# Products issued ahead of a run-time switch, scatters without order, and half of the last result sent before its last product

## The chip, the cores and the metric

The kernel runs on one core of a Trainium2 chip. The metric is the device time of one execution in microseconds; the median of several runs counts. The profile is of one execution.

## What is computed

Two blocks follow each other. The first is chunked attention over 4 batches, 8 heads and 768 positions with a head size of 64; its output, seen as 3072 tokens of 512 numbers, is the input `x` of the second. The second is a mixture of 8 experts in which each token goes to the one expert with its highest logit, and no token is dropped:

```python
expert_idx = np.argmax(x @ w_gate, axis=1)
for e in range(E):
    h = np.maximum(x_sorted[lo:hi] @ w1[e], 0.0)
    y_sorted[lo:hi] = h @ w2[e]
y = y_sorted[inv_perm]
return (gate_w[:, None] * y).astype(np.float32)
```

`w1` of an expert is 512x1024, `w2` is 1024x512, everything is float32. How many tokens an expert gets is known only when the kernel runs.

## The kernel before

**Attention and routing** fill the first 160 us or so. Each block's rows of `x` are scattered to a table in device memory, `x_dram`, with 1024 places for every expert. Counts per expert are turned into `cases`: the number of tokens in steps of 32.

**The experts** are a loop over `e`. For each, `tc.Switch(index[e], CASES)` chooses at run time one of 33 bodies, written out for 0, 32, 64 ... 1024 tokens. Every engine has its own copy of the code and makes the jump for itself, from registers that `loads` filled (line 1211). The code that follows the switch is common again: `result`, then the next switch. So at each boundary an engine jumps twice: from the end of the old body to the common code, and from there into the next body.

**A body** (`expert`) takes one part of tokens, or two equal ones if there are over 512. A part of `w` tokens is split into two halves of `hf = w // 2` columns, and each layer is a product of 2x2 blocks by Strassen's scheme in Winograd's form: seven products in place of eight, on blocks and sums of blocks. Products 1 and 2 (`product(1, ...)`, `product(2, ...)`) use the blocks as they are; products 3 and 5 to 7 need sums of `x` blocks (`xS`) or sums of weight blocks (`wT`), product 4 a sum of weights. `product` runs on TensorE (line 1081) into one of six accumulator banks of 2x256 columns. Each matmul of these float32 operands gives two records in the trace, so that one product of the first layer for one half of its outputs (`p`) is 8 records.

In `first_layer` the products come in the order 1, 2 (for both `p`), 6, 7, 5, 4, 3; the bank of each is the next of six in turn. ScalarE copies product 1 (line 1107), VectorE adds product 2 to it (line 1108), ScalarE applies the ReLU (line 1100). Between them stand `backs`: the four `put_back` of the expert before. `put_back` turns 128 tokens of the result back on TensorE (`turn_y`, line 1012), scales them with the gate on ScalarE (`gated`, line 1017, four buffers `y`), and scatters their rows to the output from GpSimd (`store`, line 1021). `turns` are the transposes of the next expert's `x` (`turn_x`, lines 1006 and 1007). `second_layer` runs products 1, 4, 5, 6, 7, 2, 3; the sums for the next expert are made in `between`. Product 3 is the last, in bank 5; VectorE adds it in `result` (line 1164), after the switch. This completes the first half of the token columns of `yT`; the other half is complete two additions earlier (lines 1156 and 1158), and `put_back` with `g` of 2 and 3 reads that half.

**Order.** The whole part is written under `manual_schedule`: each engine runs its instructions as the code issues them. Waits are put in by the recording layer from what each instruction reads and writes. It sees every `store` as a write to the whole of `out`, so each scatter waits for the one before to land. The last expert's result is put back after the loop, four `put_back` one after the other (lines 1251 and 1252). Then `good`, one number that says whether the fast path was admissible, is loaded into a register on each engine (line 1261), and a branch skips the fallback `general`.

Of the kernel before, what the change touches and what calls it, by code (L numbers as in the profile page):

```python
# [26 lines left out]
N, DM, E, F = B * S, H * D, 8, 1024  # L27
# [49 lines left out]
HALF = CAP // 2  # L77
# [10 lines left out]
def parts(n):  # L88

    n1 = n if n <= CAP else STEP * -(-n // (2 * STEP))  # L90
    return [w for w in (n1, n - n1) if w]
# [419 lines left out]
def ordinary(ctx, tc, q, k, v, mem_k, mem_v, moe_w_gate, moe_w1, moe_w2, out, good):  # L511
# [503 lines left out]
    def gated(py, gate):  # L1015
        y = mpool.tile([128, DM], F32, name="y", bufs=4)
        nc.scalar.activation(y, py, AF.Copy, scale=gate)  # L1017
        return y

    def store(y, token):  # L1020
        nc.gpsimd.indirect_dma_start(  # L1021
            out=out,
            out_offset=bass.IndirectOffsetOnAxis(ap=token.bitcast(I32), axis=0),
            in_=y,
            in_offset=None,
            bounds_check=N - 1,
            oob_is_err=False,
        )

    def put_back(yT, tg, g):  # L1030

# [44 lines left out]
    def product(i, bank, w, a, q0):  # L1076

        hf, k = a[i].shape[2], a[i].shape[1]
        for q in range(2):
            for c in range(k):  # L1080
                mm(  # L1081
                    bank[:, q, 0:hf],
                    lhsT=w[i][:, c, 128 * (q0 + q) : 128 * (q0 + q) + 128],
                    rhs=a[i][:, c],
                    start=c == 0,
                    stop=c == k - 1,
                )
        return bank[:, :, 0:hf]

    def sums_of_x():  # L1090
        a = halves(xT, KX, HALF)
        sums(a, xS, slice(0, KX // 2))
        sum4(a, xS, slice(0, KX // 2))

    def first_layer(e, hf, backs, turns, new):

        a = halves(xT, KX, hf)
        w, a = weights(e, 0), streams(a, xS[:, :, :, 0:hf])
        hh, s = halves(h, KH, hf), hS[:, :, :, 0:hf]
        relu = lambda o: nc.scalar.activation(o, o, AF.Relu)  # L1100
        T = lambda i: tmp[:, i, :, 0:hf]
        C = lambda p: slice(2 * p, 2 * p + 2)
        to = lambda i, j, p: hh[i][j][:, C(p)]
        turn_of = iter(range(14))
        P = lambda i, p: product(i, banks[next(turn_of) % 6], w, a, 2 * p)
        for p in range(2):
            nc.scalar.copy(T(p), P(1, p))  # L1107
            i = add(to(0, 0, p), T(p), P(2, p), op=OP.add)
            if p == 0 and new and e + 1 < E:
                for n in range(4):  # L1110
                    fetch_w(e + 1, 0, n, after=i)
            relu(to(0, 0, p))
        for f in backs[:2]:
            f()
        for p in range(2):
            add(T(p), T(p), P(6, p), op=OP.add)
        for f in backs[2:]:
            f()
        for p in range(2):
            add(T(2 + p), T(p), P(7, p), op=OP.add)  # L1120
        if new:
            sum_weights(e, 1, (5, 6))
        for p in range(2):
            p5 = P(5, p)
            add(to(1, 1, p), T(2 + p), p5, op=OP.add)  # L1125
            relu(to(1, 1, p))
            add(T(p), T(p), p5, op=OP.add)
        if new:
            sum_weights(e, 1, (4,))
        for p in range(2):  # L1130
            add(to(1, 0, p), T(2 + p), P(4, p), op=OP.add)
            relu(to(1, 0, p))
        for f in turns[:1]:
            f()
        for p in range(2):
            sums(hh, s, C(p))
            p3 = P(3, p)
            for f in turns[1:2] if p == 0 else turns[2:]:
                f()
            add(to(0, 1, p), T(p), p3, op=OP.add)  # L1140
            relu(to(0, 1, p))
        for p in range(2):
            sum4(hh, s, C(p))
        if new:
            sum_weights(e, 1, (7,))

    def second_layer(e, hf, yT, between):
        w, a = weights(e, 1), streams(halves(h, KH, hf), hS[:, :, :, 0:hf])
        p1, u2, u3 = (tmp[:, i, :, 0:hf] for i in (0, 4, 5))
        P = lambda i, b: product(i, banks[b], w, a, 0)  # L1150
        nc.scalar.copy(p1, P(1, 2))
        between()
        p4, p5 = P(4, 3), P(5, 4)
        add(u2, p1, P(6, 0), op=OP.add)
        add(u3, u2, P(7, 1), op=OP.add)
        add(yT[:, 2:4, 1, 0:hf], u3, p5, op=OP.add)
        add(u2, u2, p5, op=OP.add)
        add(yT[:, 0:2, 1, 0:hf], u3, p4, op=OP.add)
        add(yT[:, 0:2, 0, 0:hf], p1, P(2, 2), op=OP.add)
        P(3, 5)  # L1160

    def result(yT):
# [3 lines left out]
    def expert(e, n):  # L1166


        ps = parts(n)
        both = lambda f, *x: [lambda g=g: f(*x, g) for g in range(4)]  # L1170
        backs = both(put_back, yTs[(e - 1) % 2], tgs[(e - 1) % 2]) if e else []
        yT = yTs[e % 2]
        x = xes[e % 2]
        if len(ps) == 2:
            fetch_x(xe2, e, 1)
        for k, w in enumerate(ps or [0]):
            last = k + 1 >= len(ps)
            tg = tgs[e % 2 if last else 2]
            nc.vector.tensor_copy(tg, x[:, :, DM : DM + 2])
            if k == 0 and e + 2 < E:  # L1180
                fetch_x(x, e + 2, 0)
            x = xes[(e + 1) % 2] if last else xe2
            turns = both(turn_x, x) if not last or e + 1 < E else []
            if w:
                first_layer(e, w // 2, backs, turns, k == 0)
            else:
                for f in backs + turns:
                    f()
                if e + 1 < E:
                    for i in range(4):  # L1190
                        fetch_w(e + 1, 0, i)
            if last and e + 1 < E:
                for i in range(4):
                    fetch_w(e + 1, 1, i)

            def between():
                if turns:
                    sums_of_x()
                if last and e + 1 < E:
                    sum_weights(e + 1, 0)  # L1200

            if w:
                second_layer(e, w // 2, yT, between)
            else:
                between()
            if not last:
                result(yT)
                backs = both(put_back, yT, tg)

    def loads(engines, c, n):  # L1210
        return {eng.engine: eng.value_load(cases[0:1, c : c + 1], min_val=0, max_val=n - 1) for eng in engines}

    with tc.manual_schedule():
        choose(last)
        label(last)

        w1 = ws[0][0].rearrange("p (k n) -> p k n", n=F)
        w2 = ws[0][1].rearrange("p (k n) -> p k n", n=DM)
        for g in range(2):
            turn_x(xe2, g)  # L1220
        for f in range(KH):
            ph = banks[f % 4][:, 0]
            for c in range(KX):
                mm(ph, lhsT=w1[:, c, 128 * f : 128 * f + 128], rhs=xT[:, c, 0], start=c == 0, stop=c == KX - 1)
            nc.scalar.activation(h[:, f, 0], ph, AF.Relu)
            if f == 1:
                rank(last, banks[4].rearrange("p a b -> p (a b)"))()
                count_up(banks[5])
                scatter(sent, NB)
        for t in [xes[1]] + yTs:  # L1230
            nc.vector.memset(t, 0.0)
        engines = (nc.tensor, nc.scalar, nc.vector, nc.gpsimd, nc.sync)
        index = [loads(engines, e, CASES) for e in range(E)]
        fetch_x(xes[0], 0, 0)
        fetch_x(xes[1], 1, 0)
        sum_weights(0, 0)
        for g in range(2):
            py = banks[4 + g].rearrange("p a b -> p (a b)")
            for f in range(KH):
                mm(py, lhsT=h[:, f, 0, 128 * g : 128 * g + 128], rhs=w2[:, f], start=f == 0, stop=f == KH - 1)  # L1240
            if g == 0:
                for g2 in range(4):
                    turn_x(xes[0], g2)
                sums_of_x()
            y = gated(py, xe2[:, g, DM + 1 : DM + 2])
            store(y, xe2[:, g, DM : DM + 1])
        for e in range(E):
            for a in tc.Switch(index[e], CASES):  # L1248
                expert(e, STEP * a)
            result(yTs[e % 2])  # L1250
        for g in range(4):
            put_back(yTs[(E - 1) % 2], tgs[(E - 1) % 2], g)


@with_exitstack
def kernel(ctx, tc, *args):
    nc = tc.nc
    gpool = ctx.enter_context(tc.tile_pool(name="gpool", bufs=1))
    good = gpool.tile([1, 1], I32, name="good")
    ordinary(tc, *args, good)  # L1260
    rv = nc.values_load(good[0:1, 0:1], min_val=0, max_val=1)  # L1261
    with tc.If(rv == 0):
        general(tc, *args)

# [27 lines left out]
```

## Time and profile before

| | before |
|---|---|
| median of three runs | 609.12 us (604.49 to 613.68) |
| span of the profiled execution | 597.4 us |
| TensorE matmul busy | 521.7 us, 87% |
| TensorE weight load busy | 497.3 us, 83% |
| VectorE busy | 324.2 us, 54% |
| ScalarE busy | 175.8 us, 29% |
| GpSimd busy | 135.0 us, 23% |
| mean granted TensorE clock | 0.942 |

Busy shares are means over a span with different stages. The expert stage lasts from about 200 us to the end. Taken from the records of line 1081, the half widths `hf` of the bodies in this input are 144, 112, 224, 192, 144 twice (one expert in two parts), 160, 96 and 256 columns. A granted clock of 1.00 is full speed. In the trace, PEld is TensorE's weight load, PEldq the sequencer that feeds TensorE, and a matmul's end is modelled.

### The profile page before, as it was taken

Reading aid. Unit: us, or ns where it says so; the run is one execution under the profiler, and the core shown is the slowest. Engines: PE = TensorE matmul, PEld = TensorE weight load, DVE = VectorE, ACT = ScalarE, POOL = GpSimd, SP = SyncE. Lnnn points to the kernel's source line nnn. Section 1 sums busy time; section 2 is a strip of 40 time slices with the busy share of each in tenths; the row PEclk is TensorE's granted clock in tenths of the full one; section 3 lists DMA queues with packets and bytes.
Section 4 is the critical chain, followed back from the end, with each engine's and each line's share of the span. In section 5 each row is a group of like instructions: output and inputs, shape, how many; then the busy total and the mean of one; then the engine's idle time right before and its main releaser. Section 6 shows DMA issues by size and latency. Waiting matters only on the chain. (4 is left out here: it accounts for less than half of the span.)

```text
span 597.4 us, 10606 instructions
## 1 busy us (share of the span) xinstructions
PE 521.7 (87%) x3850; PEld 497.3 (83%) x3850; DVE 324.2 (54%) x757; ACT 175.8 (29%) x414; POOL 135.0 (23%) x174
## 2 busy tenths in 40 slices
PE   4999999999898997978997998999979799699900
PEld 3999999999885797978997997999879799588700
DVE  4556666656445394671872692755719548165300
ACT  3556556564221230402400320405023031122010
POOL 3500222312456310313201323211032011020020
PEclk9999999999789998997998998999989999799965
DMA  9999999996232370824311732403246063000010
GB/s 173 182 179 167 229 213 232 257 209 149 78 109 84 106 282 7 314 71 158 130 69 26 268 116 59 184 9 110 81 160 235 11 234 103 5 24 2 3 72 1
DMA packets 81658, 76.17 MB, mean 128 GB/s; under 512 B 39852, under 2 KB 64556, under 8 KB 81456
## 3 DMA queue, kind: packets, MB, share of 16 engines
q1 hardware_dynamic: 72368, 54.54, 38.4%
q0 software_dynamic: 8128, 19.29, 9.8%
q8 instruction: 55, 0.90, 0.7%
q14 instruction: 147, 1.20, 0.7%
q10 hardware_dynamic: 960, 0.24, 0.2%
HBM read 65.04 MB, written 16.45 MB: 136 GB/s over the span
## 5 line engine op out<-in xcount | busy, mean ns | idle before, releaser
L1021 POOL DMA_INDIRECT out_dram<-y,tg x36 | 40.5, 1126 | 194.1 <-ACT y L1017 100.1
L1081 PE MATMUL b<-xT,w 128*128 128x144 f32 (+6 forms) x288 | 56.3, 368 | 29.2 <-issue 25.7
L1081 PEld LDWEIGHTS b<-xT,w 128*128 128x128 f32 x288 | 52.6, 238 | 33.0 <-issue 31.1
L1100 ACT ACTIVATE h<-h 128x288 f32<-128x288 f32 (+6 forms) x72 | 33.7, 476 | 94.6 <-DVE h L1125 45.5
L686 PE MATMUL o<-v,ex 128*96 128x65 f32 x512 | 54.9, 251 | 1.0 <-PE o L686 1.0
L1107 ACT COPY big<-b 128x288 f32<-128x288 f32 (+6 forms) x18 | 7.7, 430 | 152.0 <-PE b L1081 151.6
L686 PEld LDWEIGHTS o<-v,ex 128*96 128x96 f32 x512 | 51.3, 167 | 1.1 <-issue 1.1
L662 PE MATMUL sc<-qT,kT 128*128 128x192 f32 x256 | 49.7, 339 | 0.0
L675 ACT ACTIVATE ex<-sc,cst 128x256 f32<-128x256 f32 x96 | 38.3, 470 | 31.5 <-PE sc L662 31.1
L825 POOL DMA_INDIRECT xe<-x_dram,rows x38 | 40.4, 1062 | 25.0 <-PE b L1081 13.1
L1081 PE MATMUL b<-xS,w 128*128 128x144 f32 (+6 forms) x288 | 45.6, 307 | 0.0
L1081 PE MATMUL b<-big,w 128*128 128x144 f32 (+6 forms) x288 | 44.4, 307 | 0.0
L1081 PE MATMUL b<-xS,wT 128*128 128x144 f32 (+6 forms) x288 | 44.3, 307 | 0.0
L1081 PE MATMUL b<-h,w 128*128 128x144 f32 (+6 forms) x288 | 44.3, 307 | 0.0
L1081 PE MATMUL b<-big,wT 128*128 128x144 f32 (+6 forms) x288 | 42.9, 307 | 0.0
L662 PEld LDWEIGHTS sc<-qT,kT 128*128 128x128 f32 x256 | 42.7, 197 | 0.0
L1081 PEld LDWEIGHTS b<-big,w 128*128 128x128 f32 x288 | 41.5, 190 | 0.8
L1081 PEld LDWEIGHTS b<-h,w 128*128 128x128 f32 x288 | 41.3, 190 | 0.8
L1081 PEld LDWEIGHTS b<-xS,w 128*128 128x128 f32 x288 | 41.3, 191 | 0.8
L1081 PEld LDWEIGHTS b<-xS,wT 128*128 128x128 f32 x288 | 41.2, 190 | 0.8
L1081 PEld LDWEIGHTS b<-big,wT 128*128 128x128 f32 x288 | 41.0, 190 | 0.8
L1057 DVE TENSOR_TENSOR wT<-w,wT 128x1024 f32<-128x1024 f32 x32 | 39.1, 1223 | 0.8
(150 smaller groups left out, 829.7 us busy)
## 6 DMA issues: line engine op xcount, KB each, us to landing
w<-in_moe_w_dram SPq DMA_DIRECT2D x64, 512.0 KB
kn<-in_k_dram SPq DMA_DIRECT2D x16, 384.0 KB
qn<-in_q_dram SPq DMA_DIRECT2D x16, 384.0 KB
v<-in_v_dram SPq DMA_DIRECT2D x24, 128.0 KB
v<-in_v_dram SPq DMA_DIRECT2D x24, 112.0 KB
v<-in_v_dram SPq DMA_DIRECT2D x8, 144.0 KB
v<-in_v_dram SPq DMA_DIRECT2D x8, 96.0 KB
xe<-x_dram,rows POOLq DMA_INDIRECT x38, 4.1
```

The source lines that it names most:

```text
L662: mm(sc[:, 2 * a : 2 * a + 2, 0:QB].rearrange("p x (j t) -> p x j t", j=2), lhsT=turned[b][:, a, w0 : w0 + WIN], rhs=units[i // 2]["qT"][: ...
L675: nc.scalar.activation(ex4[:, :, :, sl], sc4[:, :, :, sl], AF.Exp, bias=mask[:, 3 * x + g : 3 * x + g + 1], scale=D**-0.5)
L686: mm(o[:, j], lhsT=s["ex"][:, h], rhs=s["v"][:, h], start=True, stop=True)
L825: nc.gpsimd.indirect_dma_start(out=to.bitcast(I32), out_offset=None, in_=x_dram, in_offset=bass.IndirectOffsetOnAxis(ap=which, axis=0), bo ...
L1021: nc.gpsimd.indirect_dma_start(out=out, out_offset=bass.IndirectOffsetOnAxis(ap=token.bitcast(I32), axis=0), in_=y, in_offset=None, bounds ...
L1057: add(w[i], *of[i], op=OP.subtract)
L1081: mm(bank[:, q, 0:hf], lhsT=w[i][:, c, 128 * (q0 + q) : 128 * (q0 + q) + 128], rhs=a[i][:, c], start=c == 0, stop=c == k - 1,)
L1100: relu = lambda o: nc.scalar.activation(o, o, AF.Relu)
L1107: nc.scalar.copy(T(p), P(1, p))
```

## The change

Three things are changed, and a load is moved.

1. A new function `lead` issues products 1 and 2 for both `p` before the switch, in the common code. As the width of the coming body isn't known there, it takes the whole half of 256 columns; columns past `hf` are computed and not read. In the body, `P` only names the bank for these four. The aim is that TensorE has work in its queue while its sequencer jumps. The second part of an expert with two parts still runs all its products in the body.
2. `store` declares that it doesn't depend on the other stores in the list `stores`, since the tokens differ. The list is emptied at the start of each body and after each switch.
3. In the last expert, `put_back` of `g` 2 and 3 stands before product 3, in the body; only `g` 0 and 1 are left for the end.
4. `good` is loaded into registers before the expert loop, next to the loads of `cases`.

```diff
+    stores = []
+
     def store(y, token):
-        nc.gpsimd.indirect_dma_start(
+        i = nc.gpsimd.indirect_dma_start(
...
+        for j in stores:
+            tc.declare_no_dep(i.ins, j, reason="rows of different tokens")
+        stores.append(i.ins.name)
...
+    def lead(e):
+
+        a, w = streams(halves(xT, KX, HALF), xS), weights(e, 0)
+        for p in range(2):
+            product(1, banks[2 * p], w, a, 2 * p)
+            product(2, banks[2 * p + 1], w, a, 2 * p)
...
-        P = lambda i, p: product(i, banks[next(turn_of) % 6], w, a, 2 * p)
+
+        def P(i, p):
+            bank = banks[next(turn_of) % 6]
+            return bank[:, :, 0:hf] if new and i < 3 else product(i, bank, w, a, 2 * p)
+
...
         add(yT[:, 0:2, 0, 0:hf], p1, P(2, 2), op=OP.add)
+        if e + 1 == E and last:
+            for g in (2, 3):
+                put_back(yT, tgs[e % 2], g)
         P(3, 5)
...
         ps = parts(n)
+        del stores[:]
...
         index = [loads(engines, e, CASES) for e in range(E)]
+        in_range = nc.values_load(good[0:1, 0:1], min_val=0, max_val=1)
...
         for e in range(E):
+            lead(e)
             for a in tc.Switch(index[e], CASES):
                 expert(e, STEP * a)
+            del stores[:]
             result(yTs[e % 2])
-        for g in range(4):
+        for g in range(2):
             put_back(yTs[(E - 1) % 2], tgs[(E - 1) % 2], g)
+    return in_range
```

More of the change, by code (lines that the diff above doesn't have):

```diff
@@ L1145, in first_layer, with second_layer @@
             sum_weights(e, 1, (7,))
-    def second_layer(e, hf, yT, between):
+    def second_layer(e, hf, yT, between, last):
         w, a = weights(e, 1), streams(halves(h, KH, hf), hS[:, :, :, 0:hf])
@@ L1202, in expert @@
             if w:
-                second_layer(e, w // 2, yT, between)
+                second_layer(e, w // 2, yT, between, last)
             else:
                 between()
+                if e + 1 == E:
+                    for g in (2, 3):
+                        put_back(yT, tg, g)
             if not last:
@@ L1259 @@
     good = gpool.tile([1, 1], I32, name="good")
-    ordinary(tc, *args, good)
-    rv = nc.values_load(good[0:1, 0:1], min_val=0, max_val=1)
+    rv = ordinary(tc, *args, good)
     with tc.If(rv == 0):
```

## The prediction

> **What bounds the kernel now.** I read the page first: TensorE is busy for 87% of the span and weight loads for 83%, VectorE for 54%, so TensorE is the candidate, and the question is where its other 13% lie. The list of waits, TensorE alone, answers:
>
> ```profile
> PE b L1081 <- issue: 25.7, 6, 5.6
> PE b L1081 <- DVE yT L1164: 3.4, 1, 3.4
> ```
>
> Columns: total us, times, longest. Seven waits, 29.1 us, all at the first product of a body (line 1081), six with no releaser at all. "Issue" means that nothing in the data held TensorE. The timeline of TensorE shows one such place (start, duration, what, idle before it), and the sequencer's own instructions in the same stretch show what it was doing (min/median/max ns, first and last start):
>
> ```profile
> 263.27 1.95 PE L1081 MATMUL b<-big,w 128*128 128x112 f32 x16
> 270.81 8.54 PE L1081 MATMUL b<-xT,w 128*128 128x224 f32 x32 [5.59 <-issue]
> 279.19 1.04 PE L1012 MATMUL ty<-cst,yT 128*128 128x128 f32 x8
> L1287 PEldq COMPARE_BRANCH  x2: 2597/3537/4477, 263.1 to 266.1; - x2
> L1287 PEldq MOVE  x2: 29/32/34, 265.8 to 265.9; - x2
> ```
>
> Two jumps: one out of the old body (from 263.1, 2.60 us), one into the chosen body (from 266.1, 4.48 us). The first was reached while 16 to 17 matmuls were still queued (TensorE worked until 265.2), so it is mostly covered; the second has nothing queued ahead of it. The same count, 17 matmuls left when the first jump starts, stands at all seven boundaries. Third, the stretches around it (busy us and count of each engine, then the granted clock, DMA share, GB/s):
>
> ```profile
> 265.20:270.80 5.60, 0.02 (x1) 0.02 (x1) 0.69 (x1) 0.00 (x0) 0.00 (x0) 0.80 0.06 10
> 270.80:279.20 8.40, 8.39 (x33) 7.94 (x34) 0.79 (x2) 1.64 (x3) 4.10 (x5) 0.73 0.27 70
> 279.20:297.80 18.60, 18.60 (x113) 18.41 (x112) 12.87 (x20) 7.08 (x13) 4.68 (x5) 1.00 0.52 195
> ```
>
> After the gap the clock is 0.73 for the first products, then 1.00. So a boundary costs twice: the gap, and slow first products. Last, the tail, from the timeline:
>
> ```profile
> 567.63 0.98 POOL L1021 DMA_INDIRECT out_dram<-y,tg  x1 [32.57 <-ACT y L1017]
> 573.22 0.98 POOL L1021 DMA_INDIRECT out_dram<-y,tg  x1 [4.61 <-DMA out_dram<-y,tg]
> 576.75 0.98 POOL L1021 DMA_INDIRECT out_dram<-y,tg  x1 [2.55 <-DMA out_dram<-y,tg]
> 580.26 0.98 POOL L1021 DMA_INDIRECT out_dram<-y,tg  x1 [2.53 <-DMA out_dram<-y,tg]
> ```
>
> The last four scatters run one after the other, each released by the landing of the one before. TensorE is done at 568.6; the end is at 597.4.
>
> [...] 4.26 to 5.12 us for each of the eight jumps into a body on TensorE. [...] the trace shows about 33 entries (17 matmuls, 16 weight loads) left when a jump starts, and I use the trace. [...] gaps of 2.95 us already lowered it, while the 1.72 us gap at 182.8 did not (1.00 in both stretches after it).
>
> **The change, part by part.**
>
> *Leads at boundaries 1 to 7.* The 32 matmul records of products 1 and 2 leave the body and stand between the two jumps, 256 columns wide whatever the body's width. Before, gap plus the time from the first record to the next group: 3.44+5.26, 5.59+8.38, 3.17+6.95, 2.95+5.67, 4.53+5.91, 4.06+5.25, 5.42+9.62, in all 76.2 us. After: 32 records of 256 columns at full clock take 6.91 us (16 take 3.45 at 544.48). When the last of them is handed over, about 16.5 records of 0.216 us, 3.56 us, are still queued; the sequencer then needs 0.28 us of register work, 4.64 us of jump (mean of the seven) and 0.30 us to the first matmul, 5.22 us. Remaining gap 1.66 us. The jump out of the old body is covered by the queue except at one boundary (2.60 us against 2.2), 0.2 us on average. So 7 x (6.91+1.66+0.2) = 61.4 us: a saving of 14.8 us. In it lie about 15 us of columns that no narrow body needs (6.91 less twice the 16-record time of each width, such as 1.79 at 112 columns), paid back by the covered jump and the full clock.
>
> *Lead of the first expert.* There the jump is already hidden (no gap at 200.66) and 32 records take 3.92 us. After: 6.91 plus a gap of 1.3 (its jump is 4.26), so 4.3 us lost.
>
> *Who else waits.* The new first TensorE work of a body, the transposes of line 1012, needs the sum of line 1164. VectorE did that 0.1 to 2 us after the old body's last product and entered the next body at most 6.7 us after it; TensorE now arrives after 8.6. Queued behind these transposes are product 6 and the rest of the body; I cost the wait at nothing. Banks 0 to 3, which the lead writes, are read for the last time at line 1159 at the latest, which ends before the last product does (264.96 against 265.2). Bank 5, still to be read by line 1164, is not among them.
>
> *The register load moved to the front.* One more load among nine of about 0.3 us in the sequencer, ahead of line 1240 in a place where TensorE idles: 0.4 us at most lost. At the end it was beside other work.
>
> *Scatters without order, inside a body.* 43.9 us of GpSimd waits shrink, but GpSimd's queue holds only scatters and gathers for two experts ahead, and TensorE waits for neither. Nothing.
>
> *The tail.* 16 transposes (1 us) move ahead of the last product. The last half's y would be ready near 563.2 and 563.9, its scatters at 563.5 and 565.0. The first scatter after the body still waits for all earlier ones: 565.0 plus the longest landing, 4.8, plus 0.5 of issue is 570.3; GpSimd's jump (2.5 us at 536.4) ends before that. The last scatter, free of it, follows at the spacing of free-running ones, 1.45: 571.8 instead of 580.3. Saving 8.5 us. Bounds: 10.2 if the landing is 2.7, 6 if GpSimd's own bookkeeping (2.3 us at 534.1) comes on top. The 17.1 us after the last scatter stay.
>
> Sum: -14.8 + 4.3 + 0.4 - 8.5 = -18.6. One gap (the last, with its jump of 5.12 us, 2.1 us long) may still lower the clock, 1.7 us for a 3.4 us stretch at half clock: -16.9. On the median of 609.1 that gives **592.2 us**.
>
> **Rivals.**
> - *All jumps hidden.* If the queue covers the whole jump, boundaries cost 7 x 7.11 = 49.8, saving 26.4, and the first lead costs 3.0: -26.4+3.0+0.4-8.5 = -31.5, 577.6 us. [...] Against: 17 matmuls left, eight times.
> - *The clock still falls at every gap.* -18.6 + 8 x 1.7 = -5.0, 604.1 us. For it: gaps of 2.95 us do it, and nothing between 1.72 and 2.95 is shown. Against: 1.72 us did not.
> - *The tail gives nothing.* The 8.9 us drain that GpSimd shows at the end may have an end of its own, or the scatters may queue elsewhere: 600.7 us.
> - *Slower.* If the jump waits until the lead has run, the whole 5.2 us gap and the slow clock come on top of the wide lead: 7 x (6.91+5.2+0.2+1.7) = 98.1, +21.9; first expert +9.9; +0.4; tail -8.5: +23.7, 632.8 us. Against: the jump into the first body ran while 16 matmuls were queued.
>
> **How the numbers follow.** Forecast 0.57; all hidden 0.12; clock falls 0.15; tail nothing 0.11; slower 0.05. The runs of before spread from 604.5 to 613.7, about 4.5 us to each side, which every case inherits. Range 577 to 606: it takes in the clock rival and half of the fully hidden one, and leaves out the slower case. Faster by over 2% is below 596.9: most of the forecast (0.50), all of the hidden case, a little of the tail's: 0.65. Within 2%: 0.31. Slower: 0.04.
>
> **What would show it.** At each boundary TensorE should show 32 records of 256 columns directly after the last product, about 6.9 us, then a gap near 1.7 us, then line 1012's transposes at clock 1.00. Right: the waits on "issue" fall from 29 to about 14 us with the new one of the first expert; the last two scatters stand 1.5 us apart. Wrong: gaps of over 2.5 us or a clock near 0.7 after them; VectorE or ScalarE named as releaser of a body's first transposes; the last scatter later than 12 us after the last product.

## The result and the profile after

The changed kernel takes 583.24 us (579.72 to 587.14), the kernel before in the same comparison 609.46 us. The ratio is 0.960, 95% interval 0.950 to 0.970: faster, by about 26 us where 17 were forecast. Ratios, here and below, are taken over the fast executions alone and times are medians of all, so the quotient of two times can differ from their ratio by up to 0.007.

Busy shares first, from the head of the page of after:

```profile
PE 534.9 (91%) x3850; PEld 503.9 (86%) x3850; DVE 323.7 (55%) x757; ACT 175.8 (30%) x414; POOL 133.9 (23%) x174
```

TensorE is busy for 13 us *longer* than before (521.7 us) although the kernel is shorter. Of these, 3.3 us lie ahead of the first lead. In the expert stage 9.8 us remain: the columns that nobody reads cost some 18 us by estimate (eight leads of 6.91 us, less the same records at the width of each body), stops inside the bodies, shown below, add some slow matmuls, and first products that no longer run at a low clock take part of it back. The kernel is shorter because TensorE idles less. The waits of TensorE in after (total us, times, longest), the two that concern the expert stage most:

```profile
PE tx L1006 <- ACT xT L1007: 6.7, 5, 3.0
...
PE b L1086 <- issue: 3.6, 6, 0.9
```

"Issue" fell to 3.6 us (line 1086 is 1081 of before), and none of its six waits stands at a boundary, as will be seen. The same boundary as in the prediction, from TensorE's timeline, and the sequencer's jumps there (min/median/max ns, first and last start):

```profile
280.06 1.95 PE L1086 MATMUL b<-big,w 128*128 128x112 f32 x16
281.85 7.09 PE L1086 MATMUL b<-xT,w 128*128 128x256 f32 x32
289.26 1.07 PE L1012 MATMUL ty<-cst,yT 128*128 128x128 f32 x8 [0.32 <-PE b L1086]
```
```profile
L1314 PEldq COMPARE_BRANCH  x2: 324/2066/3807, 279.9 to 285.2; - x2
```

The lead of 32 records follows the last product without a gap, and 0.32 us after it the new body begins. The jump out took 0.32 us, the jump in 3.81 us. The windows around the lead and behind it (busy and count of PE, PEld, DVE, ACT, POOL; clock; DMA share; GB/s) show full clock:

```profile
281.80:289.20 7.40, 7.14 (x34) 5.96 (x33) 1.57 (x4) 1.53 (x3) 0.25 (x2) 1.00 0.12 14
289.20:307.80 18.60, 18.54 (x111) 18.38 (x112) 12.62 (x20) 6.99 (x13) 8.88 (x8) 1.00 0.64 223
```

From the first lead record to the next group, the seven boundaries take 7.26, 7.41, 7.02, 6.94, 6.93, 7.08 and 7.25 us, in all 49.9 (76.2 before); the first expert's lead takes 6.98 (3.92 before). Together -23.3 us.

The tail, from GpSimd's timeline:

```profile
560.87 0.98 POOL L1023 DMA_INDIRECT out_dram<-y,tg  x1 [31.92 <-ACT y L1017]
562.82 0.98 POOL L1023 DMA_INDIRECT out_dram<-y,tg  x1 [0.96 <-POOLq L1274]
569.01 0.98 POOL L1023 DMA_INDIRECT out_dram<-y,tg  x1 [5.22 <-ACTq L1289]
570.30 0.98 POOL L1023 DMA_INDIRECT out_dram<-y,tg  x1 [0.30 <-issue]
```

Two scatters now start before the body ends, the last two stand 1.29 us apart. From the last product of all to the end of the span it is 21.7 us, 32.0 before; 0.9 of these 10.3 us are transposes that moved ahead of the last product, so 9.4 are gained.

These gains, 33 us, are more than the two spans differ by (597.4 and 585.4). Two things stand against them. In this profile the first lead starts at 208.0 us and the first expert's products of before at 200.7, though little is changed ahead of them; in two other profiles of after it started at 201.9 and 205.0, and in three kernels without the load of `good` there ((1) to (3) below) the first products started between 204.4 and 208.1, so this is the spread of that part. And inside two bodies, after has stops that before hasn't. The timeline of TensorE, second body:

```profile
255.95 0.92 PE L1086 MATMUL b<-xT,wT 128*128 128x112 f32 x6
257.33 0.70 PE L1086 MATMUL b<-xT,wT 128*128 128x112 f32 x4 [0.46 <-issue]
258.79 0.59 PE L1086 MATMUL b<-xT,wT 128*128 128x112 f32 x4 [0.77 <-issue]
260.24 0.56 PE L1086 MATMUL b<-xT,wT 128*128 128x112 f32 x2 [0.85 <-issue]
...
266.91 1.97 PE L1006 MATMUL tx<-cst,xe 128*128 128x128 f32 x8 [2.22 <-ACT xT L1007]
```

Product 4 (`xT` with a sum of weights), which before ran in one piece, comes in four, and a little later the transposes of line 1006 wait for ScalarE. The windows of the same stretches, columns as above:

```profile
248.80:255.90 7.10, 7.05 (x64) 7.08 (x65) 1.13 (x3) 2.96 (x5) 5.28 (x6) 1.00 0.98 383
255.90:260.60 4.70, 2.62 (x19) 2.37 (x19) 0.73 (x3) 0.00 (x0) 2.54 (x3) 0.92 0.51 161
260.60:268.70 8.10, 5.88 (x34) 5.70 (x34) 7.84 (x18) 3.40 (x8) 0.00 (x0) 0.71 0.76 249
```

While TensorE stutters, ScalarE does nothing and VectorE almost nothing. Afterwards VectorE has a backlog (7.84 us of 8.10), TensorE waits for it through ScalarE, and the clock falls to 0.71 in that window. It happens while GpSimd sends the four scatters one after the other:

```profile
254.13 1.03 POOL L1023 DMA_INDIRECT out_dram<-y,tg  x1 [0.52 <-issue]
255.47 1.01 POOL L1023 DMA_INDIRECT out_dram<-y,tg  x1 [0.31 <-ACT y L1017]
256.78 0.98 POOL L1023 DMA_INDIRECT out_dram<-y,tg  x1 [0.31 <-issue]
258.11 0.98 POOL L1023 DMA_INDIRECT out_dram<-y,tg  x1 [0.35 <-issue]
```

The same pattern stands near 387 us, with the other three waits on "issue". Idle time of TensorE outside the boundaries is 10.7 us, 2.7 before, and three stretches of 3.4 us run at half clock, worth another half of each: about 13 us. So -23.3 - 9.4 + 13 + 7.4 = -12.3, about the 12.0 us between the spans.

### The profile page after: what moved, and what is told of

Read it like the earlier page. It is cut to its first block, busy times and chain, and to the rows that moved or that the text cites. A ratio compares the mean times of both kernels' runs of the same rounds, so it can differ in the third digit from the quotient of the medians.

```text
span 585.4 us, 10593 instructions
## 1 busy us (share of the span) xinstructions
PE 534.9 (91%) x3850; PEld 503.9 (86%) x3850; DVE 323.7 (55%) x757; ACT 175.8 (30%) x414; POOL 133.9 (23%) x174
## 5 line engine op out<-in xcount | busy, mean ns | idle before, releaser
L1023 POOL DMA_INDIRECT out_dram<-y,tg x36 | 39.0, 1084 | 135.3 <-ACT y L1017 115.6
L1086 PE MATMUL b<-xT,w 128*128 128x256 f32 (+1 forms) x288 | 60.7, 369 | 0.0
L1086 PE MATMUL b<-h,w 128*128 128x144 f32 (+6 forms) x288 | 46.6, 317 | 0.0
L1086 PEld LDWEIGHTS b<-h,w 128*128 128x128 f32 x288 | 43.7, 201 | 0.8
L689 DVE RECIPROCAL inv_all<-o 96x4 f32<-96x4 f32 x64 | 11.4, 178 | 55.9 <-PE o L686 47.5
```

Source lines behind the costliest of these rows:

```text
L689: nc.vector.reciprocal(inv, o[:, :, D])
L1023: i = nc.gpsimd.indirect_dma_start(out=out, out_offset=bass.IndirectOffsetOnAxis(ap=token.bitcast(I32), axis=0), in_=y, in_offset=None, bo ...
L1086: mm(bank[:, q, 0:hf], lhsT=w[i][:, c, 128 * (q0 + q) : 128 * (q0 + q) + 128], rhs=a[i][:, c], start=c == 0, stop=c == k - 1,)
```

## The experiments

Two questions: what each part gives alone, and what makes the stops. **Theory A**: the scatters without order make them. **Theory B**: the leads make them. For the last experiment a third was added, **Theory C**: they need the free scatters and besides a chip, or a moment, whose transfers are slower. There are three sets of runs, each on its own chip: (1) to (4), (5) and (6), and (7). All ratios are to the kernel before in the same set; intervals are of 95%. The kernel before took 608.6 us in the first set, 601.4 in the second and 607.6 in the third. The expectations say "call" for such a set.

**1. Leads alone.** To the kernel before are added only `lead(e)` before the switch, the function itself, and

```diff
+        def P(i, p):
+            bank = banks[next(turn_of) % 6]
+            return bank[:, :, 0:hf] if new and i < 3 else product(i, bank, w, a, 2 * p)
```

> The kernel before with the leads alone; scatters, tail and register load as before. In the profile of the changed kernel the eight leads with what gap is left take 56.9 us where gap and first products took 80.1, but two bodies (the second and the fifth) lose about 13 us in their middle, where TensorE and VectorE stop on 'issue' and 'remote' while the DMA engines are at 0.98. Theory A: these stops come from four scatters that no longer wait for each other, on top of the weight fetch, and starve the fetch of instructions. Then this kernel has no such stops and takes 23 us less than before, ratio 0.962. Theory B: they come from the lead, which brings the weight fetch closer to the code of the body. Then the stops are here too and the gain is about 10 us, ratio 0.983. Both expect the tail as before, the last four scatters 3.5 us apart or more.

Measured: 0.964 (0.958 to 0.970), 582.3 us. By the ratio this is -22.1 us on 608.6, close to A's number. No stop on "issue" in any body; the idle time at the boundaries is 1.6 us in all, against 29.2 before; the tail is as before (32.2 us). The leads don't make the stops on "issue": B falls. One wait of line 1006 for ScalarE, in the second body, is 1.71 us all the same, against 0.48 in the kernel before; the end of this section comes back to it.

**2. Scatters without order alone.** Only the list `stores`, `declare_no_dep` and the two `del stores[:]`.

> The kernel before with only the scatters freed of their order, within each body and among the four at the end. All theories expect the last four scatters about 1.4 us apart, the last one 8.4 us earlier. Theory A (free scatters starve the instruction fetch) expects stops of TensorE inside one to three bodies, 3 to 13 us in all, so a net of -5 to +5 us, ratio 0.992 to 1.008. Theory B expects none and the full -8.4 us, ratio 0.986.

Measured: 0.989 (0.986 to 0.992), 601.0 us. Between the two. The last four scatters start at 582.73, 584.02, 585.31 and 586.60 us, 1.29 apart, and the tail is 23.0 us, 9.0 less than before; of that 6.9 arrive, by the ratio. Stops appear in the second body though there are no leads: 0.80, 0.13 and 0.38 us on "issue" at 256 us, then 3.49 us for ScalarE's copies. The profiled execution was one of the longer ones (605.4 us), so not every execution need have stops as long. This speaks for A, by a smaller amount.

**3. The early half alone.** `put_back` of `g` 2 and 3 before product 3 of the last expert, `range(2)` at the end, scatters in order.

> The kernel before with only the early put_back of the last expert's second half; every scatter still waits for the one before. Two scatters then stand before the end of the last body, two after: the last one starts near 575.5 instead of 580.3 (565 for the third last landing, then 3.5 each), so 4 to 5 us less, ratio 0.992. If the order of scatters were what sets the tail alone, the gain would be near the time of two scatters, 7 us; if the end of TensorE sets it, nothing.

Measured: 0.993 (0.990 to 0.996), 603.2 us: as expected. The tail is 25.8 us, but its last two scatters still stand 3.5 us apart, each behind the landing of the one before.

**4. The change, with scatters free only at the end.** The declaration is made only around the last expert's own four `put_back`:

```diff
-        for j in stores:
+        for j in stores if free[0] else []:
```

> The changed kernel, but scatters inside the bodies wait for each other as before; only the last expert's own four are free. Theory A: the stops inside bodies are gone, 23 us of the leads and 9 us of the tail remain, 32 us less than before, ratio 0.947, and 8 us less than the changed kernel as profiled. Theory B: as the changed kernel, ratio 0.960, with the same stops in the second and fifth body.

Measured: 0.950 (0.945 to 0.955), 576.3 us: near A's number (0.947), and no stop on "issue" in any body. By the ratio this is -30.3 us on 608.6: 22.1 from the leads, as in (1), and 8.2 from the tail. The first result, 0.960 in another comparison, is 5.8 us worse on the same base (0.9597 less 0.9502). But one long wait is left, in the second body. VectorE and TensorE there:

```profile
253.64 0.39 DVE L1137 TENSOR_TENSOR big<-big,b 128x224 f32<-128x224 f32 x1 [3.26 <-PE b L1086]
```
```profile
261.09 1.97 PE L1006 MATMUL tx<-cst,xe 128*128 128x128 f32 x8 [2.53 <-ACT xT L1007]
```

The first line is the addition of product 7. Its operand was complete at 251.4 us, so VectorE starts 2.2 us late though the scatters are in order; the wait of 2.53 us follows from its backlog, and the clock is at half from 260.42 to 267.25 us.

**5. The change once more, and with a later weight fetch.** The second set, on the next chip, was to tell what in the free scatters stops the engines. The first kernel is the changed one unaltered; in the second the fetch of the next expert's `w1` stands behind product 5 rather than 2, away from the scatters:

```diff
-            i = add(to(0, 0, p), T(p), P(2, p), op=OP.add)
-            if p == 0 and new and e + 1 < E:
+            add(to(0, 0, p), T(p), P(2, p), op=OP.add)
...
-            add(to(1, 1, p), T(2 + p), p5, op=OP.add)
+            i = add(to(1, 1, p), T(2 + p), p5, op=OP.add)
+            if p == 0 and new and e + 1 < E:
```

> The changed kernel once more, beside the three others of this call. Ratio 0.960 to the kernel before, and again stops of TensorE inside one to three bodies while scatters and weight fetch run together, most likely in the second and the fifth body.

> The changed kernel with free scatters, but the next expert's first weights are fetched only once product 5 has been added, about 9 us later, when the four scatters of a body are out. Theory A (scatters and weight fetch together starve the fetch of instructions): no two of them at once, so no stops while the scatters run, and about 8 us less than the changed kernel, ratio 0.947 to 0.952, unless the later weights hold up VectorE's sums, which would show as waits of its weight sums for a DMA. Theory A2 (free scatters alone are enough[...]): the stops remain, ratio 0.960. Theory A3 (the weight fetch alone is enough, wherever it lies): stops move to a later place in the body.

Measured: 0.944 (0.940 to 0.948), 567.3 us, and 0.942 (0.939 to 0.946), 565.5 us. The first was a miss: the same kernel shows no stop here (the longest wait inside a body is 0.48 us), so the second has nothing to cure and tells nothing of the cause. The timelines of TensorE and GpSimd in the second body of the unaltered kernel, and its window:

```profile
249.98 1.95 PE L1086 MATMUL b<-xT,wT 128*128 128x112 f32 x16
```
```profile
247.95 1.03 POOL L1023 DMA_INDIRECT out_dram<-y,tg  x1 [0.52 <-ACT y L1017]
249.28 1.53 POOL L1023 DMA_INDIRECT out_dram<-y,tg  x1 [0.31 <-issue]
251.11 0.98 POOL L1023 DMA_INDIRECT out_dram<-y,tg  x1 [0.31 <-issue]
252.40 1.96 POOL L1023 DMA_INDIRECT out_dram<-y,tg  x1 [0.30 <-issue]
```
```profile
246.00:254.00 8.00, 8.00 (x75) 8.00 (x74) 6.09 (x12) 2.21 (x5) 6.23 (x6) 1.00 1.01 344
```

Four free scatters, the DMA engines as full as in the first result (1.01), and TensorE busy for all 8 us. So free scatters and full DMA engines, even together, are not enough.

**6. Half and quarter leads, scatters in order inside bodies.** The lead is cut to products 1 and 2 of the first `p`, or to product 1 of it; the rest stays in the body at its own width.

```diff
-        for p in range(2):
-            product(1, banks[2 * p], w, a, 2 * p)
-            product(2, banks[2 * p + 1], w, a, 2 * p)
+        product(1, banks[0], w, a, 0)
+        product(2, banks[1], w, a, 0)
```

> Scatters in order inside bodies, and only products 1 and 2 of the first p in the lead: 16 records instead of 32, the others back in the body at its own width. If what covers the jump is the queue of 16 matmuls, as the count of matmuls left says, 16 wide ones cover as much as 32: gaps stay at 0 to 0.4 us, and half of the needless columns, 8.9 us over eight boundaries, are saved: 567 us, ratio 0.936. Rival: the whole lead is needed, since the other engines' jumps take as long and the body's first products wait for them; then new waits on VectorE or ScalarE appear at the body's start, and the ratio stays near 0.950.

> As the half lead, but only product 1 of the first p, 8 records. At the start of the second jump 8 wide and about 8 narrow matmuls are left, 2.6 to 3.4 us of work against 4.1 us of register work, jump and start: gaps of 0.7 to 1.5 us, in all about 9 us, against another 4.4 us of columns saved. Net 4 us more than the half lead, ratio 0.943. The clock stays at 1.00 after these gaps, as they are under 1.72 us. If the jumps get longer again with so little between them (4.4 to 5.1 us as in the kernel before), gaps of 1.5 to 2.5 us and some stretches at half clock: ratio 0.955.

Measured: half 0.931 (0.927 to 0.935), 559.0 us; quarter 0.943 (0.940 to 0.946), 566.4 us. With the half lead the boundary's gaps are still 0 to 0.35 us, 0.86 in all. When the jump into the body starts, 15 or 16 records are left to run, which are the lead alone, and they cover it; with the full lead of 32 it was 16 as well, so the sequencer doesn't run further ahead with the longer one. With a lead of 8 records, 15 or 16 are left as well at most boundaries, but only eight of them are wide, and they don't cover the jump: 0.51 to 3.37 us, seven gaps. At the longest one a single record was left. TensorE's timeline at the longest, and the window after it:

```profile
416.23 1.89 PE L1086 MATMUL b<-xT,w 128*128 128x256 f32 x8
421.49 1.83 PE L1086 MATMUL b<-xT,w 128*128 128x160 f32 x7 [3.37 <-DVE tg L1201]
```
```profile
421.50:424.90 3.40, 3.40 (x14) 3.40 (x15) 0.49 (x1) 0.47 (x1) 1.16 (x2) 0.56 0.02 5
```

The clock is 0.56 after the gap of 3.37 us; after the next longest, 1.94 us, it stays at full speed.

**7. Free or ordered, full or half lead, on a third chip.** Two factors crossed, four kernels on one chip.

> The changed kernel, third time, in one call with the three others of a two by two: full or half lead, scatters inside bodies free or in order. Theory A (free scatters cost inside the bodies by starving the instruction fetch): slower than the same kernel in order by 4 us or more, with stops in the profile. Theory C (the stops belong to a chip or a moment with slower transfers, and free scatters only make them likelier): no stops and within 2 us of the kernel in order where the kernel before takes about 601 us, stops and 4 to 8 us where it takes about 609.

> Full lead, scatters inside bodies in order. Theory A: 4 us or more below the changed kernel of this call. Theory C: within 2 us of it on a chip where the kernel before takes about 601 us. No stops on 'issue' inside bodies in either.

> Half lead, scatters inside bodies free. 8 to 10 us below the changed kernel of this call by the columns saved, gaps at the boundaries still at most 0.4 us. Against the half lead in order: as the changed kernel against its ordered form.

> Half lead, scatters inside bodies in order: 8 to 10 us below the full lead in order, ratio 0.931 to 0.937 to the kernel before, the fastest of the four under Theory A and equal with the half lead with free scatters under Theory C.

| us (ratio, interval) | free inside bodies | ordered inside bodies |
|---|---|---|
| full lead | 581.9 (0.958, 0.954 to 0.962) | 574.6 (0.947, 0.943 to 0.951) |
| half lead | 573.7 (0.947, 0.943 to 0.952) | 567.0 (0.937, 0.933 to 0.942) |

Free scatters inside bodies cost 7.2 and 6.8 us; a half lead saves 8.1 and 7.7 us, and the two add up. The stops on "issue" are back in both free kernels and in neither ordered one. The profiles show them in the second and the fifth body, as in the first result. TensorE and VectorE of the free kernel with full leads, fifth body ("remote" is a releaser that the trace doesn't name):

```profile
378.41 0.74 PE L1086 MATMUL b<-xT,wT 128*128 128x144 f32 x4 [0.43 <-issue]
379.82 1.51 PE L1086 MATMUL b<-xT,wT 128*128 128x144 f32 x11 [0.67 <-issue]
...
387.40 1.97 PE L1006 MATMUL tx<-cst,xe 128*128 128x128 f32 x8 [3.23 <-ACT xT L1007]
```
```profile
379.86 0.82 DVE L1137 TENSOR_TENSOR big<-big,b 128x288 f32<-128x288 f32 x2 [5.27 <-remote]
```

and TensorE of the ordered one in the same body:

```profile
377.41 2.12 PE L1086 MATMUL b<-xT,wT 128*128 128x144 f32 x16
...
382.88 1.14 PE L1006 MATMUL tx<-cst,xe 128*128 128x128 f32 x8 [0.51 <-ACT xT L1007]
```

In the free kernel VectorE starts the addition of product 7 at 379.86 us, though its first half was complete at 374.78, 5.1 us earlier. TensorE, by then at product 4, stutters at the end of that time, and both go on 0.9 us after GpSimd's last scatter (377.97 to 378.95). In the ordered kernel the scatters start at 373.22, 378.14, 381.85 and 385.35 us, and in this body TensorE runs on.

**What the cause of the stops is stays partly open.** Shown: TensorE's stops on "issue" go away when only the order of the scatters is restored, in (4) and in (7), there with both leads; they don't need leads (2); they don't come on every chip (5). Not shown: that free scatters alone make VectorE late. The addition of product 7 or the one before it in the second body starts late in every kernel of (1) to (4) and of (7): by up to 1.8 us in (3), which has neither leads nor free scatters, by 2.2 us in (4) and 2.6 us in the ordered kernel with full leads of (7). In that body the free kernels are late by 1.1 to 3.9 us, no more than the ordered ones on the chip of (7). In the fifth body, though, the free kernels with leads are late by 5.1 to 5.3 us and the ordered ones by at most 2.1. On the chip of (5) and (6) no such addition is late. So on some chips free scatters lengthen a delay that is there without them, and add the stops of TensorE. What they cost can also be the clock alone: in (7) TensorE with half leads idles for 8.4 us among the experts with free scatters and for 8.6 us in order, but with free scatters two stretches of 3.4 us run at half clock, in order none.

A's further idea in the expectations, that the scatters starve the fetch of instructions, is not supported: in the free kernel of (7) neither of the queues that the profile calls "instruction" (q8 and q14, 0.6% and 0.7% of the DMA engines' time in after) starts a packet during a stop. Around the later stop q8 starts none from 372.83 to 389.07 us and q14 none from 367.74 to 414.66; around the earlier one q8 none from 249.09 to 263.49 and q14 none from 243.98 to 258.72. In the first trace of the changed kernel q8 starts none from 251.28 to 268.88 and from 380.83 to 397.12 us and q14 none from 375.74 to 421.63, but around the earlier stop q14 starts one at 259.21. (7) doesn't tell A from C, as C too expected stops on a chip where the kernel before takes about 609 us (607.6 here). But C's slower transfers don't show: the packets of q1, which carry the weights, took 25.2% of the DMA engines' time from 195 to 540 us in that kernel and 24.7% in the same kernel of (5) (25.1% in the first trace of after). No run here names what holds VectorE and TensorE both.

One rival was not tested, the recording of the trace itself. The five traces without late additions (before, and the four of (5) and (6)) hold 6527 to 6554 semaphore updates; the nine with them hold fewer, 5654 to 5689 where scatters in the bodies are in order and 5248 to 5351 where they are free. Whether the recording holds the engines, or what holds them loses the records too, stays open.

## Why the prediction was right, and where it was not

The range and the direction held, but the forecast's own number was 9 us too high, and the boundaries behaved as a rival said that had been given 0.12. By its steps:

- **Leads at boundaries 1 to 7: right in kind, too small.** Forecast 61.4 us for the seven, measured 49.9, which is the figure of the rival "all jumps hidden" (49.8). The term that was mis-sized is the gap, 1.66 us forecast and 0.32 at most measured. Its parts: the queue held 15 to 16 matmuls when the jump started, a little less than the 16.5 assumed, but the jump into the body took 3.32 to 3.81 us (mean of the seven 3.52) in place of 4.64. The rival's own reason, a deeper queue, was shown by no trace and was not what happened. The 0.2 us for the jump out of the old body weren't needed either: it took 0.31 to 0.32 us every time. (Nor did the 0.2 follow from its working: 0.4 us at one boundary is 0.06 on average, which makes 1 us in the sum.) Leads alone are measured at -22.1 us (1), against -10.5 for the two lead terms.
- **First expert's lead: right in kind, too large.** +4.3 forecast; 6.98 us against 3.92 is +3.1. The gap of 1.3 us in the forecast didn't come, for the reason just given.
- **Who else waits, nothing: right at the boundaries.** No first transposes of a body are released late by VectorE; the largest wait of this kind, 0.6 us, stands after the last body.
- **Register load, 0.4 us:** not measured by itself; the start of the experts varies by more.
- **Scatters without order, inside a body, nothing: wrong.** This is the step that failed. It looked at GpSimd's queue alone, and argued that nobody waits for it. In (4) and (7) the freed scatters cost 6 to 7 us (5.8 across comparisons in (4), 7.2 and 6.8 side by side in (7)), through stops and a lower clock of TensorE and late work of VectorE, none of which depends on them by its data. What passes the delay on is not known.
- **The tail: right, in part by luck.** -8.5 forecast, -9.4 measured from the end of the product before last. Only 7.4 of it is the earlier last scatter, to which the forecast gave all 8.5; 2.0 is the time after it, 15.1 us in place of the 17.1 that were to stay. The 16 transposes that the forecast moves ahead of the last product are 8 in the trace, and take the 1 us that it gave them (0.9).
- **One gap that lowers the clock, +1.7:** none at a boundary did. The three slow stretches stand behind the stops inside bodies.

So two errors partly cancelled: the boundaries gave 11.5 us more than forecast and the bodies took about 6 to 7 us back. That the range held is to this extent luck: with scatters in order inside the bodies (4) took 576.3 us, just below its lower end of 577.

The experiments point to a better version: half leads, and scatters free only at the end. It is the fastest on both chips where it ran, 0.931 and 0.937, some 15 us faster than the changed kernel on the third chip and 8 on the second. What the half lead saves is columns, by this estimate: eight times 16 records of 256 columns, at 3.45 us, are 27.6 us; from start to next start the same records take 1.96, 1.78, 3.03, 2.60, 1.96, 2.18, 1.76 and 3.45 us at the widths of the eight bodies in the timeline of before, 18.7 us in all. That is 8.9 us, against 8.1 and 7.7 measured; in the ordered pair of (7) the half lead's larger gaps at the boundaries, up to 0.55 us each, take about 1.5 us back.

## What to carry to other kernels

A jump whose target isn't known was hidden here by work that is the same for all targets, placed between the two jumps; it needed only be about as long as the jump that comes after it (16 records, 3.45 us, for jumps of 3.3 to 3.9 us left gaps of at most 0.35 us in (6) and 0.55 us in (7)), half of what the change put there, since the sequencer ran no more than 17 matmuls ahead at these jumps, and the other half cost 7.7 and 8.1 us in (7). A declared independence should be given only where the wait stands on the path, here the last four scatters: removing waits elsewhere cost 6 to 7 us where it was measured, and what passes that cost on is not known. And the same kernel can show or not show such an effect on different chips, so a pair of versions must run side by side on more than one.

## What the runs showed of the hardware

- The jump itself became shorter: into a body 3.32 to 3.81 us in the changed kernel, 4.26 to 5.12 in before; out of one 0.31 to 0.32 us in the changed kernel, in before 1.02 to 2.60 at six boundaries and 0.32 and 0.33 at the other two. Over all fourteen traces it was 3.2 to 4.3 us into a body with leads, whatever their length, and 4.3 to 5.1 without (3.3 to 4.3 for the first body alone); out of one 0.30 to 0.34 us with leads, 0.8 to 2.6 at most boundaries without. Why wasn't found.
- The length of a gap doesn't tell when TensorE's clock fell: after 2.22 us in the changed kernel it did, after 2.44 us in the half lead in order of (7) it didn't (the next 16 records of line 1086 take 1.94 us, as those ahead of it in that body do). In before, the stretches at half clock among the experts start at 234.42, 268.55, 323.16, 367.54, 435.80, 476.76 and 510.90 us; five last 3.41 us, the second and the last 6.83. From one start to the next it is 10, 16, 13, 20, 12 and 10 times 3.413 us. In the changed kernel they start at 259.86, 266.69 and 396.40 us, 2 and 38 times 3.413 us apart.
- In these two traces the busy time of TensorE in stretches of that length, counted from those starts, does tell them apart. Of 199 at full clock between 200 and 563 us, the ten with at most 1.71 us of busy time were followed by half clock and the 189 with at least 2.24 us weren't. So the stretch from 256.45 to 259.86 us in the changed kernel, with 1.71 us in all, was followed by half clock, though no gap in it was over 0.85 us. Of twelve at half clock, the ten with at least 3.04 us were followed by full clock, and the two with 1.15 and 1.92 us weren't. Two stretches, columns as above: the first has most of the gap of 2.22 us in the changed kernel, and the clock fell after it; the second has most of the gap of 2.44 us in the half lead in order, and the clock stayed:

```profile
263.28:266.69 3.41, 1.40 (x13) 1.23 (x11) 3.22 (x9) 1.77 (x5) 0.00 (x0) 1.00 0.50 166
254.10:257.52 3.42, 1.89 (x17) 1.82 (x18) 3.19 (x11) 2.88 (x7) 0.87 (x1) 1.00 0.84 309
```

- The unchanged kernel took 601.4 us on one chip and 607.6 and 608.6 on two others, and the first lead of the changed one started between 201.9 and 208.0 us in its three profiles.
